# Attention with two mixtures of experts: the output rows of a chunk from three bf16 parts of x in place of two fp32r halves

## The chip, the cores and the metric

The kernel runs on one core of a Trainium2 chip. The metric is the device time of one execution in microseconds. A core has a matrix engine (PE, with its weight loads shown apart as PEld), a vector engine (DVE), a scalar engine (ACT), GpSimd (POOL) and SP, which here issues DMAs. Each engine works its own instructions strictly in their order, and they wait for one another through semaphores.

## What is computed

```python
def _attn_ref(u, v, z):                      # batch 4, sequence 2496, width 256, z of width 64
    scores = np.matmul(z, z.transpose(0, 2, 1)) / S
    attn = np.maximum(scores, 0.0) ** 2
    return u * np.matmul(attn, v)
x = attn_out.reshape(B * S, D)               # 9984 rows
# first mixture: rows with x @ w_skip > 0 get x + gate * expert(x), expert = argmax(x @ w_gate), F = 1024
# second mixture: logits = x @ w_gate2 + bias[modality]; every row gets gate * expert(x)
```

Each row of the attention's output decides three things by its product with 17 columns of weights: the 8 logits of the first mixture, the 8 of the second and the skip score. An expert is then chosen by the largest logit, so these products are made from split operands: a number is held as a rounded part and the rest, and the products of the parts are added.

## The kernel before

Attention comes first and takes the first 714 us of the execution, then the two mixtures run tile by tile over lists of rows. Attention works on chunks of 512 columns (queries); there are five to a batch of 2496 and 20 in all, the last of each batch with 448 columns. A chunk has ten units (`u` 0 to 9), each over 256 keys. For a unit, PE makes the scores `s` (`scores`, L295), ACT takes relu out of PSUM and squares (`t`, L298 and L310), DVE makes a rounded half `ah` and the rest `al` (L311, L312), and PE multiplies both with `vh` and `vl` into `o` (`values`, L350). Pairs of matmuls stand side by side on the upper and the lower 64 rows of the array. `ps_s` has one buffer, so the scores of a unit wait until relu has read those of the unit before.

`Attention.run` issues the work of all engines unit by unit: the scores of unit i, the values of a unit three earlier, the relu, square and split of unit i, then jobs (loads and splits of z and v for the next batch, steps of a plan), then `step()`, which moves each open `tail` on by one `yield`. So the order on each engine is the order of this loop, and a tail's pieces stand on each engine behind the unit's own work.

The `tail` of a chunk (L356) turns its finished `o` into rows. In the text below, slot 2 is the unit of the next chunk in which `o` becomes ready. Slot 2: `xs` joins the two halves of `o`, and x is the product with u (L365, in the tile `ut`). Slot 3: ACT rounds x into `xh`, DVE makes the rest `xl` (L372, L373; fp32r, 2 x 512 columns each). Slot 4: nothing (`later`, for all but the last two chunks). Slots 5 to 8: `rows` (L382), one group of 128 tokens each. A group is four pairs of matmuls, 98 columns each: 64 columns of the identity, which turn x into rows, and twice 17 columns of gate weights (`wg_split`: rounded, and the rest). The stationary operand is x, 128 tokens wide; the weights stream. ACT copies the turned rows into `r` and the logit parts into `lo`. Then DVE adds the logit parts (L406 to L414), finds the largest, PE counts the rows of each expert (`row_counts`, L160 to L170, bf16 matmuls with `tri` and `ones` as stationary operands and 64, 32, 32 and 16 columns), and POOL scatters the rows to lists.

The last chunk's tail is worked off after the attention loop by hooks of the first mixture's first tile (`m1.turn`): `hidden` 0 to 7 make `ph` (L833), ACT and DVE make `hh` and `hl` of it (L835, L836), and the tail's split stands behind `hidden(0)`, its first two groups of rows behind `hidden(3)`. `ph` has three buffers.

Of the kernel before, what the change touches and what calls it, by code (L numbers as in the profile page):

```python
# [23 lines left out]
E, F = 8, 1024  # L24
NM = 2
KT = 19
QC = 512
NCH = 5
# [8 lines left out]
C_G2, C_TID, C_G1, C_B2, RW = 256, 257, 258, 260, 268  # L37
# [4 lines left out]
HALVES = slice(0, 64), slice(64, 128)  # L42
# [5 lines left out]
def chunk_len(c):  # L48
    return min(QC, S - c * QC)
# [60 lines left out]
class FirstMax:  # L110


    def __init__(self, nc, pool, k, lg, P, n, tag, df=None, hot=None):
        self.nc = nc
        sh = [P, n, E]
        t = lambda name, *sh: pool.tile([128, *sh], F32, name=name + tag)[:P]
        mx = t("mx", n)
        self.df, self.hot = (t("df", n, E), t("hot", n, E)) if df is None else (df, hot)
        self.ex, self.sm = t("ex", n, E), t("sm", n)
        df, hot = self.df, self.hot  # L120
        nc.vector.tensor_reduce(mx, lg, axis=AX.X, op=ALU.max)
# [76 lines left out]
class Attention:  # L198


    def __init__(self, tc, sh, ctx, main, k, zT, v, uT, wg, lists, carry, nb):
        self.tc, self.nc, self.k, self.sh, self.nb = tc, tc.nc, k, sh, nb
        self.zT, self.v, self.uT = zT, v, uT
        self.lists, self.carry = lists, carry
        nc = self.nc

        pool = lambda c, name, bufs, **kw: c.enter_context(tc.tile_pool(name=name, bufs=bufs, **kw))
        self.p_u = pool(ctx, "p_u", 2)
        self.p_x = pool(ctx, "p_x", 1)
# [12 lines left out]
        self.zz = [sh.z, [p_ab.tile([128, 2560], F32R, name=n) for n in ("zA", "zB")]]  # L222
        self.vh, self.vl, self.o = {}, {}, {}
        self.zraw, self.vraw, self.ut = {}, {}, {}

        wr = p_w.tile([128, 2, 17], F32, name="wg_raw")
        nc.scalar.dma_start(wr, wg)
        self.wg_raw, self.wg = wr, p_w.tile([128, 2, 162], F32R, name="wg_split")

    def gate_split(self):  # L230
        nc, wr = self.nc, self.wg_raw
        for d in range(2):
            for p in HALVES:
                nc.scalar.copy(self.wg[p, d, 98 * d:98 * d + 64], self.k.ident[p, p])
        for d, c in enumerate((64, 64)):
            hi = self.wg[:, d, c:c + 17]
            nc.scalar.copy(hi, wr[:, d])
            nc.vector.tensor_tensor(self.wg[:, d, c + 17:c + 34], wr[:, d], hi.bitcast(F32), op=ALU.subtract)


    def z(self, b):
        return self.zz[(self.nb - b) % 2]
# [113 lines left out]
    def tail(self, b, c):  # L356
        nc, k = self.nc, self.k
        n = chunk_len(c)
        o, x = self.o.pop((b, c)), self.ut.pop((b, c))
# [6 lines left out]
        if n < QC:  # L366
            nc.vector.memset(x[:, :, n:QC], 0.0)
        yield
        xh = self.p_x.tile([128, 2, QC], F32R, name="xh")
        xl = self.p_x.tile([128, 2, QC], F32R, name="xl")  # L370
        for d in range(2):
            nc.scalar.copy(xh[:, d], x[:, d])  # L372
            nc.vector.tensor_tensor(xl[:, d], x[:, d], xh[:, d].bitcast(F32), op=ALU.subtract)  # L373
        yield
        later = b * NCH + c < self.nb * NCH - 2
        if later:
            yield

        r = self.p_r.tile([128, 4, RW], F32, name="r")
        lo = self.p_s.tile([128, 2, 4, 34], F32, name="lo")  # L380

        def rows(g0, m, lo=lo):  # L382

            ps = [self.ps_m.tile([128, m, 196], F32, name="m") for _ in HALVES]
            for g in range(m):
                q = slice((g0 + g) * 128, (g0 + g) * 128 + 128)
                for d in range(2):
                    cc = slice(64 * d, 64 * d + 98)
                    for i, x in enumerate((xh, xl)):
                        for h, p in enumerate(HALVES):  # L390
                            nc.tensor.matmul(
                                ps[h][:, g, cc], x[p, d, q], self.wg[p, d, cc], start=(d == i == 0),
                                stop=(d == i == 1), skip_group_check=True,
                            )
            gs = slice(g0, g0 + m)
            to = r[:, gs, 0:D].rearrange("p g (d h c) -> p g d h c", d=2, h=2)
            for h, t in enumerate(ps):
                nc.scalar.copy(to[:, :, :, h], t.rearrange("p g (d c) -> p g d c", d=2)[:, :, :, 0:64])
                nc.scalar.copy(lo[:, h, gs], t[:, :, 64:98])

        m = 2 if b * NCH + c == self.nb * NCH - 1 else 1
        for g in range(0, 4 - m, m):
            rows(g, m)
            yield
        rows(4 - m, m)
        nc.vector.tensor_tensor(lo[:, 0], lo[:, 0], lo[:, 1], op=ALU.add)  # L406
        lo = lo[:, 0]
        lg = self.p_s.tile([128, 2, 4, E], F32, name="lg")
        sk = self.p_s.tile([128, 4], F32, name="sk")
        for s in range(2):  # L410
            nc.vector.tensor_tensor(lg[:, s], lo[:, :, s * 8:s * 8 + 8], lo[:, :, 17 + s * 8:25 + s * 8], op=ALU.add)
        nc.vector.tensor_tensor(sk, lo[:, :, 16], lo[:, :, 33], op=ALU.add)
        gi = b * GPB + 4 * c
        nc.vector.tensor_tensor(lg[:, 1], lg[:, 1], k.bias[:, gi:gi + 4], op=ALU.add)  # L414
        nc.gpsimd.tensor_copy(r[:, :, C_B2:C_B2 + E], lg[:, 1])
        yield
        fm = FirstMax(nc, self.p_s, k, lg.rearrange("p s g e -> p (s g) e"), 128, 8, "a")
# [15 lines left out]
        at = row_index(nc, self.p_s, rks, ohb, self.carry, 128, 2, 4, "a")  # L433
# [12 lines left out]
    def run(self, first, inits, late):  # L446
# [927 lines left out]
```

## Time and profile before

| | us |
|---|---|
| median of 3 runs | 1476.23 (1475.93 to 1477.01) |
| the profiled execution | 1476.05 |
| its span, first to last instruction | 1474.2 |
| PE busy | 1459.5 (99%) |
| DVE busy | 1070.8 (73%) |
| ACT busy | 946.6 (64%) |
| mean granted TensorE clock | 0.999 of 2.4 GHz |

The profile was read in this order: busy shares by stage, then the waits of PE, then the order of time around one group of rows, around one `row_counts` and around the split of one tail. Rows of the order of time give start (us from the span's start), duration (us), engine, line, what is written and read, and in brackets the idle time before and what ended it; consecutive rows of one kind are merged (x2), so that a pair of matmuls is one row. Starts of matmuls are what is compared here, since their durations overlap.

### The profile page before, as it was taken

Reading aid. Unit: us, or ns where it says so; the run is one execution under the profiler, and the core shown is the slowest. Engines: PE = TensorE matmul, PEld = TensorE weight load, DVE = VectorE, ACT = ScalarE, POOL = GpSimd, SP = SyncE. Lnnn points to the kernel's source line nnn. Section 1 sums busy time; section 2 is a strip of 40 time slices with the busy share of each in tenths; the row PEclk is TensorE's granted clock in tenths of the full one; section 3 lists DMA queues with packets and bytes.
Section 4 is the critical chain, followed back from the end, with each engine's and each line's share of the span. In section 5 each row is a group of like instructions: output and inputs, shape, how many; then the busy total and the mean of one; then the engine's idle time right before and its main releaser. Section 6 shows DMA issues by size and latency. Waiting matters only on the chain. (4 is left out here: it accounts for less than half of the span.)

```text
span 1474.2 us, 35153 instructions
## 1 busy us (share of the span) xinstructions
PE 1459.5 (99%) x10985; PEld 1263.7 (86%) x10985; DVE 1070.8 (73%) x2540; ACT 946.6 (64%) x1721; POOL 509.8 (35%) x788
## 2 busy tenths in 40 slices
PE   9999999999999999999999999999999999999998
PEld 7988888888888888888889999998888888888886
DVE  8888888888888888787887777777555555555553
ACT  8877777777777787776556666654554545545453
POOL 2011111111111111111356556655535445354454
PEclk9999999999999999999999999999999999999999
DMA  6411211112111140011345655554433344334440
GB/s 231 180 41 56 80 38 42 44 59 73 37 43 44 58 145 31 29 61 45 99 140 182 184 185 179 180 173 131 172 133 129 132 153 140 132 129 132 154 140 28
DMA packets 46370, 161.00 MB, mean 109 GB/s; under 512 B 12118, under 2 KB 12821, under 8 KB 37056
## 3 DMA queue, kind: packets, MB, share of 16 engines
q1 hardware_dynamic: 29232, 124.57, 26.0%
q0 software_dynamic: 16896, 35.11, 6.8%
q8 instruction: 62, 1.02, 0.3%
q14 instruction: 36, 0.29, 0.1%
q10 hardware_dynamic: 144, 0.02, 0.0%
HBM read 124.57 MB, written 36.21 MB: 109 GB/s over the span
## 5 line engine op out<-in xcount | busy, mean ns | idle before, releaser
L350 PE MATMUL o<-ah,vh 64*128 64x512 f32 (+1 forms) x1560 | 313.6, 384 | 0.1
L350 PE MATMUL o<-al,vh 64*128 64x512 f32 (+1 forms) x1560 | 306.8, 383 | 0.0
L350 PE MATMUL o<-ah,vl 64*128 64x512 f32 (+1 forms) x1560 | 304.9, 382 | 0.0
L836 DVE SCALAR_TENSOR_TENSOR hl<-ph,hh 128x512 fp32r<-128x512 f32 (+1 forms) x288 | 176.3, 613 | 146.3 <-ACT hh L835 138.6
L715 POOL TENSOR_TENSOR w<-w2raw,w 128x256 fp32r<-128x256 f32 x282 | 198.5, 744 | 211.1 <-issue 188.4
L737 POOL DMA_INDIRECT lists<-r,ix x80 | 102.0, 1275 | 476.5 <-ACT t L310 246.5
L312 DVE TENSOR_TENSOR al<-t,ah 128x1024 fp32r<-128x1024 f32 (+2 forms) x201 | 239.9, 1193 | 19.0
L298 ACT ACTIVATE t<-s 128x1024 f32<-128x1024 f32 (+2 forms) x201 | 201.2, 1002 | 79.5 <-PE s L295 71.8
L835 ACT ACTIVATE hh<-ph 128x512 fp32r<-128x512 f32 (+1 forms) x288 | 155.6, 540 | 100.3 <-PE ph L833 92.7
L833 PE MATMUL ph<-mxh,zA 128*128 128x512 f32 (+1 forms) x576 | 209.3, 363 | 3.1 <-DVE hl L836 1.6
L310 ACT ACTIVATE t<-t 128x1024 f32<-128x1024 f32 (+2 forms) x201 | 208.1, 1036 | 5.7
L833 PE MATMUL ph<-mxh,zB 128*128 128x512 f32 (+1 forms) x576 | 207.0, 359 | 0.0
L833 PE MATMUL ph<-mxl,zA 128*128 128x512 f32 (+1 forms) x576 | 206.8, 359 | 0.0
L311 DVE CAST ah<-t 128x1024 fp32r<-128x1024 f32 (+2 forms) x201 | 136.9, 681 | 63.0 <-ACT t L310 59.7
L350 PEld LDWEIGHTS o<-ah,vh 64*128 64x128 f32 x1560 | 153.9, 184 | 28.0 <-DVE xs L363 0.5
L350 PEld LDWEIGHTS o<-al,vh 64*128 64x128 f32 x1560 | 154.0, 184 | 25.9 <-DVE al L312 0.2
L350 PEld LDWEIGHTS o<-ah,vl 64*128 64x128 f32 x1560 | 150.4, 184 | 25.9
L939 PE MATMUL o<-hh,w 128*128 128x348 f32 x512 | 124.8, 327 | 0.0
L833 PEld LDWEIGHTS ph<-mxh,zA 128*128 128x128 f32 x576 | 108.4, 188 | 19.0 <-DVE hl L836 3.1
L820 ACT CAST mxh<-m 128x512 fp32r<-128x512 f32 (+1 forms) x72 | 37.9, 526 | 134.6 <-PE m L816 83.4
L295 PE MATMUL s<-zA,zB 64*128 64x512 f32 (+1 forms) x400 | 123.9, 386 | 0.0
L295 PE MATMUL s<-zB,zA 64*128 64x512 f32 (+1 forms) x400 | 121.6, 387 | 0.0
(240 smaller groups left out, 3012.8 us busy)
## 6 DMA issues: line engine op xcount, KB each, us to landing
w1raw<-in_w SPq DMA_DIRECT2D x36, 1024.0 KB
w2raw<-in_w SPq DMA_DIRECT2D x36, 1024.0 KB
x_in<-lists SPq DMA_DIRECT2D x20, 536.0 KB
vraw<-in_v SPq DMA_DIRECT2D x20, 512.0 KB
ut<-in_uT SPq DMA_DIRECT2D x20, 512.0 KB
lists<-x_in POOLq DMA_DIRECT2D x16, 536.0 KB
x_cur<-lists SPq DMA_DIRECT2D x16, 351.8 KB
x_in<-lists SPq DMA_DIRECT2D x15, 351.8 KB
```

The costliest lines, as they stand in the source:

```text
L295: nc.tensor.matmul(s[:, i, :n], w[p, k], x[p, q], start=(j == 0), stop=(j == 2))
L298: nc.scalar.activation(t[:, i, :n], s[:, i, :n], AF.Relu, scale=SCALE)
L310: nc.scalar.activation(t[:, i, :n], t[:, i, :n], AF.Square)
L311: nc.vector.tensor_copy(h[:, i, :n], t[:, i, :n])
L312: nc.vector.tensor_tensor(l[:, i, :n], t[:, i, :n], h[:, i, :n].bitcast(F32), op=ALU.subtract)
L350: nc.tensor.matmul(o[half][d][:, :n], w[p, d * 128:d * 128 + 128], x[p, :n], start=(u == 0 and j == at[0]), stop=(u == 9 and j == at[-1]),)
L715: lo_engine.tensor_tensor(l[:, c], src[:, c], h[:, c].bitcast(F32), op=ALU.subtract)
L737: i = tc.nc.gpsimd.indirect_dma_start(out=out, out_offset=bass.IndirectOffsetOnAxis(ap=ix, axis=0), in_=rows, in_offset=None, bounds_check ...
L833: nc.tensor.matmul(ps, w, x, start=(i == 0), stop=(i == len(mms) - 1))
L835: nc.scalar.activation(h, ps, AF.Relu)
L836: nc.vector.scalar_tensor_tensor(l, ps, 0.0, h.bitcast(F32), op0=ALU.max, op1=ALU.subtract)
L939: nc.tensor.matmul(self.y[d], w[:, dd], h[f], start=(f == 0 and i == 0), stop=(f == 7 and i == 2))
```

## The change

The split of x now makes three bf16 parts, each of a whole 128x1024 tile: `xb0` is x rounded (ACT), x is lessened by it in place (DVE), `xb1` is the remainder rounded (ACT), `xb2` the second remainder (DVE, written as bf16). There is a `yield` between the two halves of this work, except for the last chunk, and the empty step `later` is gone from its place, so that the second half stands in slot 4. The gate weights are three bf16 parts too. A part i of x is multiplied with the first 3 - i parts of the weights, so a group of rows is six pairs of matmuls with 115, 98 and 81 columns, for each of two halves of the width; the logit parts of both halves of the width add up in PSUM. The sums of the logit parts are one reduction in place of four additions.

```diff
-        self.wg_raw, self.wg = wr, p_w.tile([128, 2, 162], F32R, name="wg_split")
+        self.wg_raw, self.wg = wr, p_w.tile([128, 2, 179], BF16, name="wg_split")
...
-        for d, c in enumerate((64, 64)):
-            hi = self.wg[:, d, c:c + 17]
-            nc.scalar.copy(hi, wr[:, d])
-            nc.vector.tensor_tensor(self.wg[:, d, c + 17:c + 34], wr[:, d], hi.bitcast(F32), op=ALU.subtract)
+        for i in range(3):
+            for d in range(2):
+                w = self.wg[:, d, 64 + 17 * (i if d == 0 else 2 - i):][:, 0:17]
+                nc.scalar.copy(w, wr[:, d])
+                if i < 2:
+                    nc.vector.tensor_tensor(wr[:, d], wr[:, d], w, op=ALU.subtract)
...
-        xh = self.p_x.tile([128, 2, QC], F32R, name="xh")
-        xl = self.p_x.tile([128, 2, QC], F32R, name="xl")
-        for d in range(2):
-            nc.scalar.copy(xh[:, d], x[:, d])
-            nc.vector.tensor_tensor(xl[:, d], x[:, d], xh[:, d].bitcast(F32), op=ALU.subtract)
-        yield
-        later = b * NCH + c < self.nb * NCH - 2
-        if later:
-            yield
+        at = b * NCH + c
+        later = at < self.nb * NCH - 2
+        xs3 = [self.p_x.tile([128, 2, QC], BF16, name=f"xb{i}") for i in range(3)]
+        for i in range(2):
+            nc.scalar.copy(xs3[i], x)
+            nc.vector.tensor_tensor(x if i == 0 else xs3[2], x, xs3[i], op=ALU.subtract)
+            if i or at < self.nb * NCH - 1:
+                yield
+        both = [(d, i, m, 64 + 17 * (3 - i)) for d in range(2) for i, m in enumerate(xs3)]
...
-                for d in range(2):
-                    cc = slice(64 * d, 64 * d + 98)
-                    for i, x in enumerate((xh, xl)):
-                        for h, p in enumerate(HALVES):
+                for d, i, x, n in both:
+                    cc = slice(0, n) if d == 0 else slice(179 - n, 179)
+                    for h, p in enumerate(HALVES):
...
-        nc.vector.tensor_tensor(lo[:, 0], lo[:, 0], lo[:, 1], op=ALU.add)
-        for s in range(2):
-            nc.vector.tensor_tensor(lg[:, s], lo[:, :, s * 8:s * 8 + 8], lo[:, :, 17 + s * 8:25 + s * 8], op=ALU.add)
-        nc.vector.tensor_tensor(sk, lo[:, :, 16], lo[:, :, 33], op=ALU.add)
+        nc.vector.tensor_reduce(
+            both17, lo.rearrange("p g h (a c) -> p g c (h a)", c=17), axis=AX.X, op=ALU.add
+        )
```

On DVE, the split of the seventh chunk's tail stood behind one unit's `ah` and `al` (slot 3), and slot 4 had only its own pair:

```order
L365 TENSOR_TENSOR ut<-ut,xs 128x1024
L311 CAST ah<-t 128x1024
L312 TENSOR_TENSOR al<-t,ah 128x1024
L373 TENSOR_TENSOR xl<-ut,xh 128x512 x2
L311 CAST ah<-t 128x1024
L312 TENSOR_TENSOR al<-t,ah 128x1024
L311 CAST ah<-t 128x1024
```

Now the same place holds one subtraction behind slot 3's pair and another behind slot 4's:

```order
L366 TENSOR_TENSOR ut<-ut,xs 128x1024
L312 CAST ah<-t 128x1024
L313 TENSOR_TENSOR al<-t,ah 128x1024
L376 TENSOR_TENSOR ut<-ut,xb_4033 128x1024
L312 CAST ah<-t 128x1024
L313 TENSOR_TENSOR al<-t,ah 128x1024
L376 TENSOR_TENSOR xb_4035<-ut,xb_4034 128x1024
L312 CAST ah<-t 128x1024
```

What moved is the making of the last part: one slot later, between slot 4's `al` and slot 5's `ah`.

On PE, the first group of rows of that chunk was four pairs between the last values of slot 5 and the next scores:

```order
L350 MATMUL o_3904<-al,vh 128x512
L391 MATMUL m<-wg_split,xh 128x98 x2
L391 MATMUL m<-wg_split,xl 128x98 x2
L391 MATMUL m<-wg_split,xh 128x98 x2
L391 MATMUL m<-wg_split,xl 128x98 x2
L295 MATMUL s<-zA 128x512
```

Now it is six pairs at the same place, each matmul with a weight load of its own in the program; half of them, the first half of the width, read:

```order
L351 MATMUL o_4000<-al,vh 128x512
L390 LDWEIGHTS xb_4033
L390 MATMUL m<-wg_split,xb_4033 128x115
L390 LDWEIGHTS xb_4033
L390 MATMUL m<-wg_split,xb_4033 128x115
L390 LDWEIGHTS xb_4034
L390 MATMUL m<-wg_split,xb_4034 128x98
L390 LDWEIGHTS xb_4034
L390 MATMUL m<-wg_split,xb_4034 128x98
L390 LDWEIGHTS xb_4035
L390 MATMUL m<-wg_split,xb_4035 128x81
L390 LDWEIGHTS xb_4035
```

The third pair loads the last part of x, `xb_4035`, which is the tile that DVE writes behind slot 4's `al`.

On DVE at the end of attention, the last chunk's product and split before:

```order
L363 TENSOR_TENSOR xs<-o_10320,xs 128x448
L365 TENSOR_TENSOR ut<-ut,xs 128x2x448
L367 MEMSET ut 128x2x64
L757 MEMSET ix_zero_scatter_10887 128x3
L758 MEMSET ix_scatter_10886 128x3
L757 MEMSET ix_zero_scatter_10906 128x4
L758 MEMSET ix_scatter_10905 128x4
L836 SCALAR_TENSOR_TENSOR hl_10864<-ph,hh_10856 128x348
L373 TENSOR_TENSOR xl<-ut,xh 128x512 x2
L836 SCALAR_TENSOR_TENSOR hl_10865<-ph,hh_10857 128x348
```

Now, where the six small operations on `sma` and `r` belong to the chunk before the last (the last two are shown):

```order
L439 TENSOR_SCALAR r<-tid_81 128x4
L440 MEMSET r 128x4
L366 TENSOR_TENSOR ut<-ut,xs 128x2x448
L368 MEMSET ut 128x2x64
L756 MEMSET ix_zero_scatter_11175 128x3
L757 MEMSET ix_scatter_11174 128x3
L756 MEMSET ix_zero_scatter_11194 128x4
L757 MEMSET ix_scatter_11193 128x4
L835 SCALAR_TENSOR_TENSOR hl_11152<-ph,hh_11144 128x348
L376 TENSOR_TENSOR ut<-ut,xb_11216 128x1024
L376 TENSOR_TENSOR xb_11218<-ut,xb_11217 128x1024
L835 SCALAR_TENSOR_TENSOR hl_11153<-ph,hh_11145 128x348
```

The six operations, which stood ahead of `xs`, now stand between it and the product, since the chunk before the last has one step more; and both subtractions, with ACT's two roundings between them, stand ahead of the second `hl`.

## Rows read from the trace of the kernel before

**Rows 1.** Busy us by stage: stretch, length; PE, PEld, DVE, ACT, POOL; clock, DMA.
```profile
60.00:705.00 645.00, 642.74 (x6111) 538.74 (x6109) 539.53 (x1142) 487.91 (x803) 100.04 (x89) 1.00 0.16 54
```
**Rows 2.** Order of time, PE: scores of a unit with nothing beside them.
```profile
71.66 0.42 PE L350 MATMUL o<-al,vh 64*128 64x512 f32 x2
...
72.59 0.42 PE L350 MATMUL o<-ah,vh 64*128 64x512 f32 x2
```
**Rows 3.** Order of time, PE: a unit with a group of rows.
```profile
55.44 0.42 PE L350 MATMUL o<-al,vh 64*128 64x512 f32 x2
55.67 0.23 PE L391 MATMUL m<-wg_split,xh 64*128 64x98 f32 x2
...
55.83 0.30 PE L391 MATMUL m<-wg_split,xh 64*128 64x98 f32 x2
55.94 0.30 PE L391 MATMUL m<-wg_split,xl 64*128 64x98 f32 x2
...
56.81 0.42 PE L350 MATMUL o<-ah,vh 64*128 64x512 f32 x2
```
**Rows 4.** Order of time, PE: a unit with `row_counts` (four bf16 pairs).
```profile
75.13 0.41 PE L350 MATMUL o<-al,vh 64*128 64x512 f32 x2
75.36 0.23 PE L160 MATMUL m<-ohba,tri 64*128 64x64 bf16 x2
...
75.48 0.47 PE L295 MATMUL s<-zB 64*128 64x512 f32 x1
...
76.25 0.42 PE L350 MATMUL o<-ah,vh 64*128 64x512 f32 x2
```
**Rows 5.** Order of time, DVE: the split of the seventh chunk's tail.
```profile
263.56 1.23 DVE L312 TENSOR_TENSOR al<-t,ah 128x1024 fp32r<-128x1024 f32 x1
264.70 1.29 DVE L373 TENSOR_TENSOR xl<-ut,xh 128x512 fp32r<-128x512 f32 x2
266.08 0.69 DVE L311 CAST ah<-t 128x1024 fp32r<-128x1024 f32 x1
266.87 1.23 DVE L312 TENSOR_TENSOR al<-t,ah 128x1024 fp32r<-128x1024 f32 x1
```
**Rows 6.** Order of time, ACT: the same tail.
```profile
262.88 1.14 ACT L372 CAST xh<-ut 128x512 fp32r<-128x512 f32 x2 [1.14 <-DVE ut L365]
263.93 1.02 ACT L298 ACTIVATE t<-s 128x1024 f32<-128x1024 f32 x1
```
**Rows 7.** Order of time, PE: scores of slot 5, then that tail's first rows.
```profile
265.00 0.50 PE L295 MATMUL s<-zA 64*128 64x512 f32 x1
...
268.55 0.21 PE L391 MATMUL m<-wg_split,xh 64*128 64x98 f32 x2
```
**Rows 8.** Order of time: the chunk before the last, whose rows wait for `xl`.
```profile
688.16 1.28 DVE L373 TENSOR_TENSOR xl<-ut,xh 128x512 fp32r<-128x512 f32 x2
688.90 0.19 PEld L391 LDWEIGHTS m<-wg_split,xl 64*128 64x128 f32 x2 [0.78 <-DVE xl L373]
...
691.73 0.23 DVE L571 TENSOR_SCALAR plan_lists<-plan_eq,plan_c 128x8 f32<-128x8 f32 x1
```
**Rows 9.** Order of time, DVE: slot 4 of the first chunk's tail.
```profile
54.93 0.82 DVE L102 SCALAR_TENSOR_TENSOR bias_tok<-mod,bia 128x640 f32<-128x640 f32 x1
```
**Rows 10.** Order of time, all engines: attention's end and the last tail's split.
```profile
712.10 0.21 DVE L133 TENSOR_REDUCE sma<-exa 128x8 f32<-128x64 f32 x1
...
713.02 0.06 DVE L441 MEMSET r<- 128x4 f32 x1
...
717.82 1.14 ACT L372 CAST xh<-ut 128x512 fp32r<-128x512 f32 x2 [1.26 <-DVE ix_scatter L758]
...
718.32 0.42 PE L833 MATMUL ph<-mxh,zA 128*128 128x348 f32 x1 [0.61 <-DVE hl L836]
...
719.76 0.50 DVE L836 SCALAR_TENSOR_TENSOR hl<-ph,hh 128x348 fp32r<-128x348 f32 x1
...
720.58 0.42 PE L833 MATMUL ph<-mxh,zA 128*128 128x348 f32 x1
```

More of the change, by code (lines that the diff above doesn't have):

```diff
@@ L233, in gate_split @@
             for p in HALVES:
-                nc.scalar.copy(self.wg[p, d, 98 * d:98 * d + 64], self.k.ident[p, p])
-        for d, c in enumerate((64, 64)):
-            hi = self.wg[:, d, c:c + 17]
-            nc.scalar.copy(hi, wr[:, d])
-            nc.vector.tensor_tensor(self.wg[:, d, c + 17:c + 34], wr[:, d], hi.bitcast(F32), op=ALU.subtract)
+                nc.scalar.copy(self.wg[p, d, 115 * d:115 * d + 64], self.k.ident[p, p])
+        for i in range(3):
[4 more added lines that the diff above has]
+                    nc.vector.tensor_tensor(wr[:, d], wr[:, d], w, op=ALU.subtract)
     def z(self, b):
@@ L368, in tail, with rows @@
         yield
-        xh = self.p_x.tile([128, 2, QC], F32R, name="xh")
-        xl = self.p_x.tile([128, 2, QC], F32R, name="xl")
-        for d in range(2):
-            nc.scalar.copy(xh[:, d], x[:, d])
-            nc.vector.tensor_tensor(xl[:, d], x[:, d], xh[:, d].bitcast(F32), op=ALU.subtract)
-        yield
-        later = b * NCH + c < self.nb * NCH - 2
-        if later:
-            yield
-        r = self.p_r.tile([128, 4, RW], F32, name="r")
-        lo = self.p_s.tile([128, 2, 4, 34], F32, name="lo")
-        def rows(g0, m, lo=lo):
-            ps = [self.ps_m.tile([128, m, 196], F32, name="m") for _ in HALVES]
+        at = b * NCH + c
+        later = at < self.nb * NCH - 2
+        r = self.p_r.tile([128, 4, RW], F32, name="r")
+        xs3 = [self.p_x.tile([128, 2, QC], BF16, name=f"xb{i}") for i in range(3)]
[5 more added lines that the diff above has]
+        both = [(d, i, m, 64 + 17 * (3 - i)) for d in range(2) for i, m in enumerate(xs3)]
+        lo = self.p_s.tile([128, 4, 2, 51], F32, name="lo")
+        def rows(g0, m):
+            ps = [self.ps_m.tile([128, m, 230], F32, name="m") for _ in HALVES]
             for g in range(m):
                 q = slice((g0 + g) * 128, (g0 + g) * 128 + 128)
-                for d in range(2):
-                    cc = slice(64 * d, 64 * d + 98)
-                    for i, x in enumerate((xh, xl)):
-                        for h, p in enumerate(HALVES):
[L391 to L394, printed above, removed]
+                for d, i, x, n in both:
+                    cc = slice(0, n) if d == 0 else slice(179 - n, 179)
+                    for h, p in enumerate(HALVES):
+                        nc.tensor.matmul(
+                            ps[h][:, g, cc], x[p, d, q], self.wg[p, d, cc], start=(d == i == 0),
+                            stop=(d == 1 and i == 2), skip_group_check=True,
+                        )
             gs = slice(g0, g0 + m)
@@ L398, in rows @@
                 nc.scalar.copy(to[:, :, :, h], t.rearrange("p g (d c) -> p g d c", d=2)[:, :, :, 0:64])
-                nc.scalar.copy(lo[:, h, gs], t[:, :, 64:98])
+                nc.scalar.copy(lo[:, gs, h], t[:, :, 64:115])
         m = 2 if b * NCH + c == self.nb * NCH - 1 else 1
@@ L405, in tail @@
         rows(4 - m, m)
-        nc.vector.tensor_tensor(lo[:, 0], lo[:, 0], lo[:, 1], op=ALU.add)
-        lo = lo[:, 0]
+        both17 = self.p_s.tile([128, 4, 17], F32, name="lg_sk")
+        nc.vector.tensor_reduce(
+            both17, lo.rearrange("p g h (a c) -> p g c (h a)", c=17), axis=AX.X, op=ALU.add
+        )
         lg = self.p_s.tile([128, 2, 4, E], F32, name="lg")
-        sk = self.p_s.tile([128, 4], F32, name="sk")
-        for s in range(2):
-            nc.vector.tensor_tensor(lg[:, s], lo[:, :, s * 8:s * 8 + 8], lo[:, :, 17 + s * 8:25 + s * 8], op=ALU.add)
-        nc.vector.tensor_tensor(sk, lo[:, :, 16], lo[:, :, 33], op=ALU.add)
+        sk = both17[:, :, 16]
         gi = b * GPB + 4 * c
-        nc.vector.tensor_tensor(lg[:, 1], lg[:, 1], k.bias[:, gi:gi + 4], op=ALU.add)
+        nc.vector.tensor_copy(lg[:, 0], both17[:, :, 0:E])
+        nc.vector.tensor_tensor(lg[:, 1], both17[:, :, E:2 * E], k.bias[:, gi:gi + 4], op=ALU.add)
         nc.gpsimd.tensor_copy(r[:, :, C_B2:C_B2 + E], lg[:, 1])
```

## The prediction, made before the changed kernel was run

> **What bounds the kernel now.** I read the busy time by stage first. From 60 to 705 us PE is busy 642.7 of 645 us at a granted clock of 1.00, its upper level, 2.4 GHz [rows 1]. DVE (540) and ACT (488) have slack on average. So attention costs what PE's stream of matmuls costs, and whatever lengthens that stream or makes it wait is lost in full; time saved on DVE or ACT counts only where PE waits for it. The reader should therefore look at two things: what a group of rows adds to PE's stream, and whether PE finds its operands ready.
>
> What a group adds is read from starts. From the last pair of values before the scores to the first pair behind them it is 0.93 us in a plain unit (71.66 to 72.59) [rows 2] and 1.37 with a group of rows (55.44 to 56.81) [rows 3]: the group adds 0.44. A pair of 512 columns takes 0.23 (55.44 to 55.67), so a column takes about a cycle at 2.4 GHz; 98 columns would be 0.041, yet the group's pairs start 0.11 apart (55.83, 55.94). Two loads of 128 columns at a cycle each, one behind the other, are 0.107: I read the group as bound by loading x, not by streaming the gate weights. Four pairs at 0.11 are the 0.44.
>
> The nearest row for bf16 operands of the same shape (64 partitions, 128 columns) is `row_counts`: its four pairs start at 75.36 and the scores follow at 75.48, 0.03 per pair, and the unit takes 1.12 (75.13 to 76.25), 0.19 more than a plain one [rows 4]. It streams 144 columns, 0.060. The rest, 0.13, is some 0.01 for each pair and about 0.10 for the scores' first fp32r load, which no longer lies beside a long stream.
>
> **The change part by part.** *Groups of rows on PE.* Six pairs of 115, 98 and 81 columns, twice, are 588 columns or 0.245 us. With 0.01 for each pair, 0.06, and the exposed load of the scores, 0.107 less the last pair's 0.034, so 0.07, a group adds 0.37 in place of 0.44. Bounds: 0.35, if the 0.01 belongs to the block and not to each pair, and 0.41 if it is 0.015 and the first load comes late too. I take 0.37, as the middle of what [rows 4] allow. 76 groups lie in the attention loop (19 chunks of four): 76 x 0.07 = **-5.2** (-2.3 to -6.8). The last chunk's two larger groups bring 0.1 at most.
>
> At this place the Trainium skill has two rules ("TensorE: Matmul & The Clock Gate"). Its section "LDWEIGHTS (loading the stationary operand)" prices a load by its columns alone, columns / 1.2 ns, whatever the type, which for 128 is 107 ns. Its section "Weight-path perf modes" says that a load of 128 columns that aren't fp32 goes faster. [rows 4] agree with the second; by the first alone the six loads would cost more than the four do now (third rival).
>
> *The last part of x.* This is the step that decides. `xl` is now ready two units ahead of its rows. In the new order DVE makes `xb2` behind slot 4's `al`. In the seventh chunk, ACT's two roundings take 1.14 from 262.88, and relu starts behind them, at 263.93 [rows 6]; the next scores, at 265.00, wait for the end of that relu (263.93 + 1.02) [rows 7]. One pass of ACT over 1024 columns takes 1.02 (that relu), so with one rounding relu and scores come about **0.10** earlier in each chunk [rows 6]. DVE's first subtraction starts at 264.70 as `xl` did (which overlaps the 1.23 of the `al` at 263.56 by 0.09) and takes 1.22 instead of 1.29. Slot 4's `al` then starts at 266.77 instead of 266.87 and ends at 268.00 [rows 5]; `xb1` is made by ACT meanwhile. The second subtraction takes 1.22 like other two-input ones of 1024 columns: 267.91 to 269.13. PE comes to the group at 268.45 (268.55 less 0.10) [rows 7] and is through with two pairs at about 268.55. A load on PE follows DVE's end within 0.10: the first half of `xl`, half of 1.28 from 688.16, is followed by a load at 688.90 [rows 8]; as the two halves overlap a little, I take 0.06. So PE starts the third pair at 269.19, after a wait of 0.64. Net of the 0.10 that is +0.54 a chunk. For 17 chunks (all but the first and the last two): **+9.2**. Bounds: 0.0 to 0.75 a chunk. DVE moves a 128x1024 tile in 0.69 where it has one input (`ah`) [rows 5], and if the subtraction with a bf16 input took that, the wait would be some 0.1 and nothing net; I take 1.22, as the subtraction still reads fp32 x beside the bf16 tile, like every 1.2 us row here.
>
> Behind the waiting load PE has the rest of the rows, the next scores, the next values. Nothing gives the time back: PE has no idle in this stage to absorb it. ACT's rounding in slot 4 (1.02) delays the next relu to some 0.9 us before PE needs it, so I cost that at nothing; were that cover gone, it would be up to 0.5 a chunk.
>
> *First chunk.* There a bias step of 0.82 (L102, from 54.93) lies on DVE between `al` and the subtraction, which then starts at about 55.67 [rows 9], so `xb2` is there for PE at 55.67 + 1.22 + 0.06 = 56.95, and PE is there at 55.77 [rows 3]: **+1.2**.
>
> *Chunk before the last.* Today its rows come one unit earlier and wait for `xl` (0.78 at the first load) [rows 8]. After the change they wait as the others do, 0.64, and for four small plan operations ahead of the subtraction (the last at 691.73; about 0.7 together): **+0.5**, between -0.8 and +1.2.
>
> *Attention's end.* Six small operations of the chunk before the last, 712.10 to 713.08, move behind `xs`, so the product, the rounding and the first `hl` come about 0.9 later, and the `ph` at 718.32, which already waits for that `hl`, comes at 719.2. ACT's first rounding moves from 717.82 to 718.75 and ends at 719.8; subtraction to 721.05; rounding to 722.1; subtraction to 723.35. The second `hl` stood at 719.76, now behind all that; the group of rows can't finish before 724.0, and the next `ph` starts then instead of at 720.58: 3.4, of which I take **+3.3** (1.5 if DVE is fast, 4 with ACT's and DVE's backlog) [rows 10].
>
> *At nothing:* one reduction in place of four additions (off PE's path, a unit before its result is used); 17 columns more in eight copies of ACT; the longer hand-over between ACT and DVE in `gate_split`, which runs once, and could cost up to 0.5 if the relu behind it comes late.
>
> **Sum** against the profiled execution's own time, 1476.05 (span 1474.2, and 0.2 under the median of 1476.23, so no correction): -5.2 + 9.2 + 1.2 + 0.5 + 3.3 = +9.0, so **1485.0**.
>
> **The rivals.** *DVE is fast on bf16.* If the second subtraction takes 0.69, the waits vanish: 17 x 0, first chunk 0.65, the one before the last 0, attention's end 2.3, and -5.2: 1473.8, within 0.2% and with the better bound of the groups (-6.8) just under it. For it: the tile is written as bf16. Against it: one input is fp32, and every two-input row of that size takes 1.2. The skill ("VectorE: DVE Perf Modes", section "The perf-mode tier table") gives two-input operations a doubled rate only with bf16 operands; no row here shows a large bf16 one.
>
> *The groups don't shrink.* If loads and streams of bf16 don't overlap, a pair costs its load of 0.03 and its stream: 0.245 + 6 x 0.03 + 0.07 = 0.495, which is 0.055 more than now: +4.2 instead of -5.2, so 1494.4. Against it, 0.03 a pair in [rows 4] contain 0.015 of stream already.
>
> *No fast load.* If x loads as slowly as now, six pairs at 0.11 are 0.66, +0.22 for each of 76 groups, +16.7 instead of -5.2: 1506.9. [rows 4] speak against it plainly.
>
> *Ready in time, gain in full.* This is the one on the faster side: if `xb2` is ready because PE reaches the group later or DVE's chain runs earlier by over 0.64, only the end of attention stays: -6.8 - 1.8 (0.10 for each of 18) + 2 = 1469.4. It decides at slot 4's `al` ending 1.3 before the group; today it ends 0.45 before it (266.87 + 1.23 to 268.55).
>
> **How the numbers follow.** The forecast has 0.74 (its own range, from the bounds of the wait, the groups and the end: 1479.5 to 1491). Fast DVE 0.10, groups that don't shrink 0.09, no fast load 0.03, ready in time 0.04. Differences under 0.2%, 3.0 us, can't be told from none. Slower by over that takes nearly all of 0.74 and the 0.12: 0.84. Same: most of the fast DVE, 0.10. Faster: 0.06. The range from 1477.0 to 1495.0 takes in the forecast's own and the groups that don't shrink, and leaves out the cheap and the dearest ends, under 0.2.
>
> **What would show it.** In the changed kernel's trace: PE waits of about 0.6 us for `xb` by the second subtraction's line, one per chunk, at the third pair of the first group alone; the three later groups of a chunk adding about 0.37 each (a unit of 1.30); both subtractions at 1.22; the scores behind slot 4 starting 0.10 earlier; a gap of about 3 us on PE near 720. It would be wrong if the waits on `xb` are under 0.2 us, if the second subtraction takes much less than 1.2, or if a later group adds more than 0.44.

## The result, and the profile after

The changed kernel takes 1489.01 us (median of 4 runs, 1488.22 to 1492.17) against 1476.62 for the kernel before beside it (4 runs, 1475.93 to 1477.76): a ratio of 1.0086, 95% interval 1.0074 to 1.0099. It is slower by 12.4 us; 9.0 were forecast (1485.0, range 1477 to 1495). The profiled execution took 1489.26, its span 1487.4, 13.2 more than the span before.

The busy time of the attention stage in the changed kernel, in the columns of [rows 1]:

```profile
60.00:705.00 645.00, 632.49 (x6348) 511.48 (x6344) 559.44 (x1098) 501.54 (x796) 96.37 (x86) 1.00 0.16 54
```

PE had been busy for 642.7 us of this stretch [rows 1] and now is for 632.5, at the same clock of 1.00: some 10 us more of waiting. What it waited for, from 60 to 740 us (releaser: us in total, times, longest):

```profile
PE m L390 <- DVE xb L376: 12.0, 18, 1.7
PE m L390 <- DVE mxl L820: 1.8, 1, 1.8
PE m L390 <- ACT xb L375: 1.6, 1, 1.6
PE s L296 <- ACT t L299: 1.1, 4, 0.3
PE ph L832 <- DVE hl L835: 0.7, 1, 0.7
```

The first line is the forecast's main term: rows of x that wait for the second subtraction (L376), once a chunk. The second, for a tile that the expert part's first transposes hold (`ps_m`, below), was in no term of it. The seventh chunk's tail again, as in [rows 5 to 7]; DVE first:

```profile
269.27 1.23 DVE L313 TENSOR_TENSOR al<-t,ah 128x1024 fp32r<-128x1024 f32 x1
270.41 1.22 DVE L376 TENSOR_TENSOR xb<-ut,xb 128x1024 bf16<-128x1024 f32 x1
```

and PE at the same place:

```profile
270.70 0.39 PE L351 MATMUL o<-al,vh 64*128 64x512 f32 x2
270.94 0.27 PE L390 MATMUL m<-wg_split,xb 64*128 64x115 bf16 x4
271.69 0.35 PE L390 MATMUL m<-wg_split,xb 64*128 64x81 bf16 x8 [0.48 <-DVE xb L376]
271.86 0.47 PE L296 MATMUL s<-zA 64*128 64x512 f32 x1
```

The subtraction ends at 271.63; two of the six pairs are through by then and the third starts at 271.69, 0.06 later, as forecast. The modelled ends of the matmuls hide a part of the wait: the profile says 0.48, but the third pair starts 0.75 behind the first, of which the two that were ready take some 0.1. That leaves the 0.64 of the forecast. A later group of the same chunk, in order of time on PE:

```profile
278.95 0.39 PE L351 MATMUL o<-al,vh 64*128 64x512 f32 x2
279.18 0.44 PE L390 MATMUL m<-wg_split,xb 64*128 64x115 bf16 x12
...
280.23 0.40 PE L351 MATMUL o<-ah,vh 64*128 64x512 f32 x2
```

From pair of values to pair of values this is 1.28, where 1.37 stood in [rows 3].

Where the rest of the 13.2 us came from is read from starts: I took the same event of PE in both traces (the first scores of a unit, the hidden products behind the attention) and subtracted. After is later by 0.1 us at unit 10, 0.8 at unit 20, 2.0 at unit 30, 5.3 at unit 190, 7.5 at unit 199, 10.0 behind the first rows of the last tail, 11.2 two hidden products later, 11.6 at 747 us, 13.0 at 1,455 and 13.2 at the end.

### The profile page after: what moved, and what is told of

The parts are those of the page before. It is cut to its first block, busy times and chain, and to the rows that moved or that the text cites. A ratio compares the mean times of both kernels' runs of the same rounds, so it can differ in the third digit from the quotient of the medians.

```text
span 1487.4 us, 35623 instructions
## 1 busy us (share of the span) xinstructions
PE 1456.5 (98%) x11305; PEld 1238.9 (83%) x11305; DVE 1097.9 (74%) x2502; ACT 965.6 (65%) x1725; POOL 512.7 (34%) x788
## 5 line engine op out<-in xcount | busy, mean ns | idle before, releaser
L1106 PE MATMUL o<-w,hh 128*128 128x512 f32 x320 | 121.2, 407 | 0.0
## 6 DMA issues: line engine op xcount, KB each, us to landing
lists<-x_in POOLq DMA_DIRECT2D x16, 536.0 KB, 12.5
```

The costliest lines, as they stand in the source:

```text
L1106: nc.tensor.matmul(self.y[g][:P], self.hh[f][:, gg], w.rearrange("p t d -> p (t d)"), start=(f == 0), stop=False)
```

## The experiments

Shifts and times below are against the kernel before in the same way. **W** is the theory of the prediction (the waits for the last part cost it), **S** its rival (bf16 rows cost more on PE themselves).

### The waits

> The changed kernel, but the third pair of a group loads xb1 again in place of xb2 (so the last part of x is left out of the rows); DVE still makes xb2, and nothing on any engine is moved. Theory W (PE's waits for xb2 are what makes the change slower): the waits go, 0.64 in most chunks, 16.1 us in all by the starts of the groups (14.0 in the first 18 chunks, 1.1 in the 19th, 1.0 in the last), and nothing else changes: 1489.0 - 15.5 = about 1473.5, under the kernel before. Rival S (the six bf16 pairs cost PE more than the four fp32r ones, or the waits only show up and would be elsewhere otherwise): above 1484.

```diff
-both = [(d, i, m, 64 + 17 * (3 - i)) for d in range(2) for i, m in enumerate(xs3)]
+both = [(d, i, xs3[min(i, 1)], 64 + 17 * (3 - i)) for d in range(2) for i in range(3)]
```

Measured: 1473.81 us (10 runs), ratio 0.9988 [0.9979, 0.9998]. The work of PE is that of the changed kernel, but no row waits for the last part. What is left of PE's waits from 60 to 700 us is 1.5 us at `ps_m`, 0.3 for `xs` and this:

```profile
PE s L296 <- ACT t L299: 1.1, 4, 0.3
```

At unit 190 it stands 6.7 us ahead of before instead of 5.3 behind; counted from unit 10, so without the start of the execution, it gains 8.3 where the changed kernel loses 5.2. That is 13.5 of the 14.0 expected there. W holds, and S, which asked for over 1484, falls.

> The kernel before with its two fp32r halves, but xl is made a unit later, where the change makes xb2. Theory W: PE waits for the second half of xl in the first group of 18 chunks, about 0.64 in most (269.46 against 268.82 in the seventh chunk), 1.2 to 1.8 in three; no part of that is won back: 1476.6 + 14 = 1490. Rival S: the place of the subtraction doesn't matter, 1477.

```diff
+later = b * NCH + c < self.nb * NCH - 2
 for d in range(2):
     nc.scalar.copy(xh[:, d], x[:, d])
-    nc.vector.tensor_tensor(xl[:, d], x[:, d], xh[:, d].bitcast(F32), op=ALU.subtract)
-yield
-later = b * NCH + c < self.nb * NCH - 2
 if later:
     yield
+for d in range(2):
+    nc.vector.tensor_tensor(xl[:, d], x[:, d], xh[:, d].bitcast(F32), op=ALU.subtract)
+yield
```

Measured: 1487.94 us, ratio 1.0087 [1.007, 1.0104], with not one bf16 row in it. The shift is +12.6 at unit 190 and +11.8 at the end, so the loss lies in the attention. PE's longest sum of waits from 60 to 740 us:

```profile
PE m L392 <- DVE xl L377: 6.0, 21, 1.2
```

(PE's weight loads, which the profile lists apart, waited 12.5 us for the same line.) A late last part is enough for such a loss; the new arithmetic isn't needed for it.

> The changed kernel with one more unit between the split and the rows (slots 6 to 9 in place of 5 to 8) for all but the last two chunks, and one unit less between the row counts and the row index, so that the lists are filled as before. Theory W: the 18 waits of the first 18 chunks go (14.0 us), the end of attention stays as it is: 1475.0. Rival S: over 1484. A third, L (rows that come later hold up what follows them, since the buffers of the tail are single): between 1478 and 1484, with new waits of PE or ACT around units 9 and 0.

```diff
             if i or at < self.nb * NCH - 1:
                 yield
+        if later:
+            yield
...
-            for _ in range(4):
+            for _ in range(3):
                 yield
```

Measured: 1477.82 us (10 runs), ratio 1.002 [1.0011, 1.003]. The waits of the ordinary chunks are gone, but scores now wait for relu, and two waits for the last part remain outside of those chunks. PE's waits from 60 to 740 us:

```profile
PE s L296 <- ACT t L299: 3.6, 12, 0.5
PE m L392 <- DVE xb L376: 2.2, 2, 1.2
```

At unit 190 it stands 6.4 us ahead of before; 6.6 of that go at the attention's end, where its rows wait as those of the changed kernel do, and the expert loop takes its 1.4. The time lies between W (1475.0) and L (from 1478). All 12 waits on relu stand ahead of the scores of slot 5; what makes relu late there I didn't trace.

### What bounds a group

> The changed kernel, but the second and third part of x are multiplied with the 64 columns of the identity alone (their products with the gate weights are left out): six pairs and twelve loads a group as before, 102 columns less of 588. If a group is bound by streaming, a later group's unit falls from 1.275 by 0.042 to 1.233 and the time by some 3 us to 1486; if by its loads or by a fixed cost for each pair, the unit stays at 1.275.

```diff
-both = [(d, i, m, 64 + 17 * (3 - i)) for d in range(2) for i, m in enumerate(xs3)]
+both = [(d, i, m, 64 if i else 115) for d in range(2) for i, m in enumerate(xs3)]
```

A group on PE, to be read beside the one above:

```profile
280.99 0.40 PE L390 MATMUL m<-wg_split,xb 64*128 64x115 bf16 x12
281.22 0.47 PE L296 MATMUL s<-zA 64*128 64x512 f32 x1
```

From the group to the scores it is 0.23 instead of 0.27 (279.18 to 279.45), and the unit is 1.235 instead of 1.275: 102 columns less are 0.040, which is what they take at 2.4 GHz (0.0425). The new group is bound by what streams. (1484.28 us in one run.)

> The kernel before, with xl multiplied only with the identity's 64 columns (its product with the gate's 34 columns is left out, twice in each group and half: 68 columns less per half). The later groups of a chunk took 1.369 us in before, 0.439 more than a plain unit (0.930). Theory L (the old group is bound by its fp32r weight loads, so columns cost nothing): the unit stays at 1.369 and the time at 1476.5. Theory S (bound by the columns that stream): 68 columns less at 2.4 GHz are 0.028 less, unit 1.341, some 2 us over 76 groups, 1474.5. The new group, which went by 0.040 for 102 columns, is bound by streaming, so if L holds here the change took the loads' bound away.

```diff
-cc = slice(64 * d, 64 * d + 98)
 for i, x in enumerate((xh, xl)):
+    cc = slice(64 * d, 64 * d + 98) if i == 0 else slice(98 * d, 98 * d + 64)
```

```profile
240.87 0.21 PE L391 MATMUL m<-wg_split,xh 64*128 64x98 f32 x2
240.91 0.26 PE L391 MATMUL m<-wg_split,xl 64*128 64x64 f32 x2
241.00 0.29 PE L391 MATMUL m<-wg_split,xh 64*128 64x98 f32 x2
241.13 0.26 PE L391 MATMUL m<-wg_split,xl 64*128 64x64 f32 x2
241.23 0.47 PE L295 MATMUL s<-zA 64*128 64x512 f32 x1
```

The unit stays at 1.37 (1.366 to 1.376 by batch, before 1.369 to 1.377) and the time at 1475.91 (one run) beside 1474.88. Starts only move within the group: theory L, the old group is bound by its loads.

### The end of the attention

> The changed kernel, only the chunk before the last forms its four groups two at a time, so that its rows end two units earlier and are out of the way of the first transposes of the expert part, which use the same two PSUM tiles. Theory C (the wait of 1.84 us ahead of the last group at 711.0 us is for those tiles): the wait is gone, the shift against before stays at about +5.4 up to the first hidden product instead of rising to +7.5, and the whole is about 1487.0. Theory R (the transposes' own operands are late because the tail's work on VectorE lies ahead of them): the wait stays, only ahead of the transposes instead, and the time remains 1489.

```diff
-m = 2 if b * NCH + c == self.nb * NCH - 1 else 1
+m = 2 if at >= self.nb * NCH - 2 else 1
```

This goes back to the second line of the waits. In the changed kernel PE does this at unit 198:

```profile
708.53 0.52 PE L815 MATMUL m<-ident,x_in 116*128 116x116 f32 x3
708.98 0.22 PE L390 MATMUL m<-wg_split,xb 64*128 64x115 bf16 x1
711.04 0.39 PE L390 MATMUL m<-wg_split,xb 64*128 64x115 bf16 x10 [1.84 <-DVE mxl L820]
```

The rows of the chunk before the last come a unit later than in before, and their last group meets the first transpose of the expert part (L815): both take tiles of `ps_m`, of which there are two. In the experiment the rows end earlier and the shift stays at +5.4 up to unit 199, as C says; but then `row_counts`, which takes a tile of `ps_m` too, waits for the same subtraction of the expert part (`mxl`, the rest of the transposed rows, which DVE makes out of the tile):

```profile
PE m L160 <- DVE mxl L820: 1.5, 1, 1.5
```

By the first hidden product the shift is 7.0 instead of 7.45, and the time 1488.58 in one run, in whose profile the clock also stays low for longer behind the last rows. So C is right that the wait is for the tiles, and not that moving these rows saves it. What keeps the tile is seen on DVE in the changed kernel:

```profile
709.46 1.09 DVE L313 TENSOR_TENSOR al<-t,ah 128x896 fp32r<-128x896 f32 x1
710.47 0.51 DVE L820 TENSOR_TENSOR mxl<-m,mxh 128x348 fp32r<-128x348 f32 x1
```

ACT's part of the transposed rows (`mxh`) is there at 709.53, and `mxl` starts 0.94 later, behind the unit's own `al`. The tail's work, which R puts there, doesn't stand ahead of it. An order with `mxl` ahead of `al` wasn't tried.

> The changed kernel with two separate edits. First, the last chunk's product with u, its casts and its subtractions are made for the two halves d=0 and d=1 one after the other, so that ScalarE and VectorE overlap. Theory P (the 2.6 us wait of the last chunk's rows is the chain of two casts and two subtractions of 1.05 and 1.22 us in single file): the wait falls to under 0.6 us, the hidden products behind it run at the full clock (0.16 us apart, not 0.29), and the shift against before just after the attention's end is +7.5 to +8.5 instead of +11.6. Rival Q (the clock falls for another reason than the idle time): the wait is gone, but the products stay 0.29 apart, shift +9.3. Second, the second expert loop's head is aligned for TensorE as the first one's is. In the changed kernel each of its turns takes 0.06 us more than in before. Theory A (where the loop's code lies): the 0.06 goes, the shift stays level over the loop, -1.4 at the end; rival: it remains, as the loop's contents are the same in both. All together 1484.5 by P and A, 1487.5 by Q without A.

```diff
+parts = (slice(0, 1), slice(1, 2)) if last else (slice(0, 2),)
...
 for i in range(2):
-    nc.scalar.copy(xs3[i], x)
-    nc.vector.tensor_tensor(x if i == 0 else xs3[2], x, xs3[i], op=ALU.subtract)
+    for d in parts:
+        to = x if i == 0 else xs3[2]
+        nc.scalar.copy(xs3[i][:, d], x[:, d])
+        nc.vector.tensor_tensor(to[:, d], x[:, d], xs3[i][:, d], op=ALU.subtract)
...
-with tc.For_i(0, n, 1, iteration_sync=mode) as j:
+with tc.For_i(0, n, 1, iteration_sync=mode, head_align_engines=(mybir.EngineType.PE,)) as j:
     m2.turn(lambda: m2.next(j), m2.finish(j))
```

(The product with u and its memset are made by halves in the same way.) The last tail's rows in the changed kernel, then the hidden products behind them:

```profile
726.98 0.23 PE L390 MATMUL m<-wg_split,xb 64*128 64x115 bf16 x2
728.77 0.22 PE L390 MATMUL m<-wg_split,xb 64*128 64x98 bf16 x2 [1.56 <-ACT xb L375]
730.03 0.61 PE L390 MATMUL m<-wg_split,xb 64*128 64x81 bf16 x20 [1.04 <-DVE xb L376]
...
731.29 0.49 PE L832 MATMUL ph<-mxh,zB 128*128 128x348 f32 x1
731.58 0.49 PE L832 MATMUL ph<-mxh,zA 128*128 128x348 f32 x1
```

The clock and the busy time in the same stretch (columns as in [rows 1]):

```profile
725.00:730.00 5.00, 1.76 (x12) 1.13 (x10) 3.25 (x10) 3.38 (x6) 3.03 (x4) 1.00 0.15 55
730.00:735.00 5.00, 4.97 (x57) 4.55 (x58) 3.16 (x7) 3.12 (x10) 1.26 (x2) 0.66 0.01 3
```

And the same place in the experiment:

```profile
725.42 0.54 PE L396 MATMUL m<-wg_split,xb 64*128 64x115 bf16 x4
726.48 0.31 PE L396 MATMUL m<-wg_split,xb 64*128 64x81 bf16 x6 [0.51 <-DVE xb L382]
727.08 0.48 PE L396 MATMUL m<-wg_split,xb 64*128 64x81 bf16 x14 [0.29 <-DVE xb L382]
...
727.77 0.32 PE L838 MATMUL ph<-mxl,zA 128*128 128x348 f32 x1
727.93 0.32 PE L838 MATMUL ph<-mxh,zB 128*128 128x348 f32 x1
```

PE waits 0.8 instead of 2.6, the products stand 0.16 apart instead of 0.29, and the shift behind them is 6.6 instead of 11.2 (1.0 of that difference was there at unit 190 already, and 0.6 more at unit 199, so that 3.0 are the edit's). P holds, with a wait of 0.8 and not under 0.6: PE was idle for most of a stretch, and in the next one stood at the lower of its two levels, 1.2 GHz, for a part of the time (0.66 in the mean). One profile would not show that such waits make the clock fall. But it fell between the end of the first wait and 0.8 us behind the second in all six profiles in which PE waits 2.6 us at this place (the changed kernel, the four orders above that start from it, and the one with the old places below), and in none of the three with the split in halves. Here the clock then fell behind a later gap (granted 0.86 and 0.80 in the two stretches of 5 us from 735, where the changed kernel has 1.00 behind the same gap), which took 1.6 us of the gain away. In all 1485.81 us. Aligning the loop's head changed nothing: its turn stays at 23.06 us, so theory A falls.

### All of it together

> The changed kernel with the four things that the runs so far point to: one unit between the split and the rows in all chunks but the last (no wait for the third part), the groups formed two at a time in all chunks (as many units as before, so the row index keeps its place), the last chunk's split in halves, and the second expert loop's head aligned. If the waits (17 x 0.64 us, the collision of 1.8, the last chunk's 2.6 and its clock) are all that stands against the gain of 76 groups (0.094 each, 7.1 us), then it is before minus 7: 1467 to 1470, and faster than both. If the wait of the scores for ScalarE that appeared with the added unit (13 x 0.3 us) grows with pairs of groups, since ScalarE then has 1.2 us of copies in one unit, 1471 to 1475. If bf16 groups gain nothing once the waits are gone, 1476.

The edits of the kernel above, and:

```diff
+        if not last:
+            yield
...
-        m = 2 if b * NCH + c == self.nb * NCH - 1 else 1
+        m = 2
...
-            for _ in range(4):
+            for _ in range(5):
```

Measured: 1465.76 us (1464.74 to 1465.99, 4 runs), ratio 0.9937 [0.992, 0.9953]: faster than both kernels, and a little more so than expected. From 60 to 705 us PE's only waits are 1.0 us for relu. Two groups in a unit, in order of time:

```profile
236.94 0.71 PE L398 MATMUL m<-wg_split,xb 64*128 64x115 bf16 x24
237.48 0.47 PE L296 MATMUL s<-zA 64*128 64x512 f32 x1
```

Two groups take 0.54 to the scores where one takes 0.27; what is saved lies around them. By starts of scores, a chunk's rows and the unit behind them cost 1.33 us more than plain units, against 1.60 for four single groups that don't wait (the order with a unit of room): each way into the bf16 rows and out costs some 0.13.

> The kernel before, two fp32r halves, with the groups formed two at a time in all chunks (the row index keeps its place). In the changed kernel two groups in a unit cost 0.48 us more than a plain unit, one alone 0.40 (3.80 against 3.40): some 0.12 of each single one was the way into and out of the rows, and pairs save that 38 times, 4.6 us. Theory E (the way in and out costs the same with fp32r): 1470.5. Theory L (the old group is bound by its own fp32r loads from end to end, 4 pairs of 0.11 us, so that two cost nearly twice as much as one): 1473 to 1475. In either case the difference to the fastest kernel so far is what the bf16 parts are worth where nothing waits.

```diff
-m = 2 if b * NCH + c == self.nb * NCH - 1 else 1
+m = 2
...
-    for _ in range(4):
+    for _ in range(6):
```

With this order the first chunk's logits are formed ahead of the last step of the token bias (61.58 and 63.88 us on DVE) and leave a part of it out, so that chunk is routed differently and the expert part isn't comparable (1619.23 us in all); only the attention is read. There a chunk of the second batch takes 35.74 us against 35.81: pairs bring the old halves nothing worth having (in the third batch, 36.09 against 35.99, they lose). Eight pairs of matmuls on PE:

```profile
236.53 0.21 PE L391 MATMUL m<-wg_split,xh 64*128 64x98 f32 x2
236.58 0.27 PE L391 MATMUL m<-wg_split,xl 64*128 64x98 f32 x2
...
237.25 0.28 PE L391 MATMUL m<-wg_split,xl 64*128 64x98 f32 x2
237.36 0.46 PE L295 MATMUL s<-zA 64*128 64x512 f32 x1
```

0.11 for each, from end to end: theory L. So in pairs the three parts are worth some 0.6 us a chunk over the two halves (35.14 against 35.74 in the second batch, where plain units take 3.400 in both), if they have the room.

### The places of the buffers

Starts of scores, unit by unit, showed a gain and a loss that no term of mine explains. Below, us from one unit's scores to the next, in a chunk of the second and of the third batch:

| slot | before, 2nd | before, 3rd | after, both | after with old places, 3rd | pairs and room |
|---|---|---|---|---|---|
| 0 | 3.400 | 3.474 | 3.400 | 3.473 | 3.521 |
| 1 | 3.521 | 3.586 | 3.521 | 3.588 | 3.486 |
| 3 | 3.400 | 3.474 | 3.400 | 3.474 | 3.400 |
| 4 | 3.622 | 3.549 | 3.532 | 3.464 | 3.531 |
| 5 | 3.919 | 3.956 | 4.462 | 4.459 | 3.549 |
| 7 | 3.880 | 3.867 | 3.800 | 3.820 | 4.066 |
| all ten | 35.81 | 35.99 | 36.03 | 36.31 | 35.14 |

Slots 0 and 3 hold no row of x in either kernel, yet the third batch gained 0.074 there; and a turn of the second expert loop, whose code is the same, went from 23.00 to 23.06. The new parts take less SBUF, so that the attention's main buffers and the expert part's lie 1,824 bytes lower.

> The kernel before, with 224 bytes left free in SBUF ahead of the buffers that the attention and the second expert loop use; nothing else. The change made its own buffers 1,824 bytes smaller, and so put those buffers elsewhere; 224 more is the same place as 1,824 less up to a multiple of 2,048. In the traces so far every kernel with the three bf16 parts has plain units of 3.400 us in all batches and 23.06 us for a turn of the second expert loop, every kernel with the two fp32r parts 3.474 in the third batch, 3.400 in the second, and 23.00. Theory D (where the buffers lie does it): this kernel shows 3.400 in both batches and 23.06, and is about 1.2 us faster than before (some 2.4 less in the first and third batch, 1.3 more in the loop): 1473.7. Theory N (it belongs to the arithmetic): 3.474, 23.00 and 1474.9 as before.

```diff
 p_w = pool(ctx, "p_w", 1)
+p_w.tile([128, 56], F32, name="pad")
```

In before, slot 0 of a chunk of the third batch:

```profile
388.26 0.39 PE L295 MATMUL s<-zA 64*128 64x512 f32 x1
...
391.74 0.39 PE L295 MATMUL s<-zA 64*128 64x512 f32 x1
```

With 224 bytes left free, the same slot, and below it a turn of the second loop:

```profile
385.69 0.39 PE L296 MATMUL s<-zA 64*128 64x512 f32 x1
...
389.09 0.39 PE L296 MATMUL s<-zA 64*128 64x512 f32 x1
```

```profile
1258.99 0.40 PE L834 MATMUL ph<-mxh,zA 128*128 128x512 f32 x1
...
1282.05 0.40 PE L834 MATMUL ph<-mxh,zA 128*128 128x512 f32 x1
```

3.40 and 23.06 instead of 3.48 and 23.00, by nothing but the places (1474.40 us in one run beside 1475.95). D holds by these paces. The whole time shows less: 1.1 of the 1.6 us between the spans were there at unit 10 already, as the granted clock rose at 5.6 us here and at 10.1 in before.

> The changed kernel with 1,824 bytes left free, so that the attention's main buffers and the expert part's lie where they lay in before: the change in arithmetic without its change of places. Theory D: plain units of the first and third batch go back from 3.400 to 3.474 and a turn of the second loop to 23.00, so the attention ends some 2.4 us later and the loop takes 1.3 less: about 1490. Theory N: 1489.0 with 3.400 and 23.06.

```diff
 p_w = pool(ctx, "p_w", 1)
+p_w.tile([128, 456], F32, name="pad")
```

```profile
392.06 0.39 PE L297 MATMUL s<-zA 64*128 64x512 f32 x1
...
395.53 0.39 PE L297 MATMUL s<-zA 64*128 64x512 f32 x1
```

The other way round: 3.47 again, and 23.00 in the loop. From unit 10 to unit 190 it loses 7.2 us where the changed kernel loses 5.2, and in the loop it doesn't lose the 1.4. The two nearly cancel (1488.85, one run, against 1489.01), so the time of the change isn't a matter of places; its parts are.

> The fastest kernel so far (pairs of groups and a unit of room), with the expert part's buffers alone put back to the addresses that they had in before. Theory D: a turn of the second loop falls from 23.06 to 23.00 us, and the whole by some 1.3 us to 1464.5; the attention keeps its 3.400. Theory N: no change, 1465.8.

```diff
+pool("moe_pad", 1).tile([128, 1824 // 4], F32, name="pad")
 p = self.p = pool("moe", 1)
```

Measured: 1468.44 us (1466.26 to 1471.07), ratio 0.9948 [0.9932, 0.9965]. The turn is 23.00, the attention keeps its 3.400, but the whole isn't faster than the 1465.76 without the edit: between the two expert loops, near 1,002 us, this profile loses 2.8 us (the one without the edit 1.2, the changed kernel none), with a granted clock of 0.66 in the 5 us from 1,005 (1.00 without the edit), and the clock falls once more near 720. Why the change of loops takes this long in some kernels stays open.

## Why the prediction was right, and where its sum was not

**Direction and mechanism** were right: the last part comes a slot late, PE has no idle time to absorb that, and it costs more than the smaller groups bring.

**The wait.** 0.64 a chunk, net 0.54, four groups less: +0.27 for an ordinary chunk. With the places held fixed it is +0.25 in the second batch (36.06 against 35.81) and +0.27 to +0.32 in the third (36.31 against 35.99 in the table). The scores behind slot 4 come 0.09 earlier (3.53 against 3.62), where 0.10 were forecast. Both subtractions take 1.219 us (median of 20 each): the rival of a fast DVE is out (its price at the attention's end stands in the prediction once as 1.5 and once as 2.3; nothing hangs on it now). The Trainium skill ("VectorE: DVE Perf Modes", section "The perf-mode tier table") asks bf16 operands for its faster rate; with one fp32 operand the trace agrees.

**The groups.** -5.2 forecast, 0.07 each. By starts of scores and with places held fixed a group's unit loses 0.08 in the second batch and 0.047 in the third, so 3.6 to 6.1 in all. The bound was read rightly on both sides: loads before (the old halves with fewer columns, and in pairs), streams after. That the two loads of a pair stand one behind the other, as the prediction has it, isn't shown: in the trace they start 0.003 to 0.03 apart, and what is measured is the 0.11 for both. The Trainium skill ("TensorE: Matmul & The Clock Gate", section "Weight-path perf modes — Fast Weight Load (FWL) and DoubleRow") says that non-fp32 loads of 128 columns go faster, and the new rows agree: six pairs with 588 columns take 0.27.

**Unit 190** was forecast at +5.4 and came at +5.3, but by errors that cancel. The buffers' new places gave 2.0, which I didn't know of. Two chunks lost about 1.0 each that I had not put there. In the second chunk the six operations of a row index of the tail before (from 92.32 to 93.52) stand ahead of the subtraction, since `step` serves the older tail first (DVE; PE's third pair comes at 94.79):

```profile
93.44 0.16 DVE L434 TENSOR_TENSOR ix<-ata,keep 128x4 int32<-128x4 f32 x1
93.52 1.22 DVE L376 TENSOR_TENSOR xb<-ut,xb 128x1024 bf16<-128x1024 f32 x1
```

In the last chunk but two, five of the plan's steps lie ahead of the subtraction (660.35 to 661.30), and I had them only in the chunk behind it, where four do (696.53 to 697.09). The first chunk cost 0.3 less than I gave it.

**The chunk before the last** was forecast at +0.5 for a wait on DVE. The waits on DVE before and after nearly cancel: the shift is +5.3 at unit 190 and +5.2 at unit 198. At unit 199 it is +7.5, and that step is the one at `ps_m`; 2.2 in all. This is the step that failed: I asked what the later subtraction delays, and not which PSUM tiles the rows hold when they come a unit later, or who else takes them there.

**The attention's end** was forecast at +3.3 and cost 2.5 in waits. The 0.9 for six small operations moved ahead of `hl` didn't come (that product waits 0.66, before 0.61 [rows 10]). But 1.2 came behind it by the clock, for which I had no term.

**The expert loop** cost 1.4 that the change's code doesn't touch, by the buffers' places.

The sum: 9.0 forecast; +1.7 for the two chunks and the first, -2.0 and +1.4 for places, +1.7 at `ps_m`, -0.8 and +1.2 at the end make 12.2 of the 13.2 in the traces; the rest is spread in steps of under 0.5.

## What to carry to other kernels

An operand that gets one more part gets one more link in its chain, so ask first in which slot the last link ends, and give the consumer a slot of room in the same edit: here that, with pairs of groups and the last split in halves, turned 12 us lost into 9 gained for the same arithmetic. Where a consumer moves by a unit, list the buffers that it holds at its new place, PSUM above all, and who takes them there. And compare plain stretches that hold no work of the change: if they move too, the places of buffers are in the difference, and a dummy tile of the same size takes them out.

## What the runs showed of the hardware

- A pair of loads of 64 rows by 128 columns with fp32r takes 0.11 us whatever streams beside it (64 or 98 columns, four pairs or eight); bf16 groups of the same shape go by their columns (102 fewer: 0.040 us less).
- The way into a stretch of the bf16 rows and out again costs some 0.13 us, so two groups in a row are worth more than one twice. With the fp32r halves it was 0.07 a chunk for two ways fewer in the second batch, and nothing in the third.
- The places of buffers in SBUF change TensorE's pace: 3.474 against 3.400 us for a unit and 23.00 against 23.06 for a turn, repeated in every kernel here whose buffers lie the one way or the other. In before the main buffers start at multiples of 64 bytes and the z of the first and third batch 32 beyond one; in after all start 32 beyond. Which operand it is, and whether 64 is the number, wasn't tried.
- Behind the 2.6 us of waiting at the attention's end the granted clock fell to 0.66 and cost 1.2 us; with 0.8 of waiting there it stayed at 1.00. Behind one and the same shorter gap (0.76 us, at the second transpose) it fell in two of the fourteen profiles and stayed at 1.00 in the others, so a term for the clock has a spread of some 2 us.
